# Two-layer MLP behind a short convolution: half-size first weight pieces, a partial band read first, clipping on GpSimd, chunk groups across batches, warming on 64 rows

## The chip, the core and the metric

The program runs on one core of one Trainium2 chip. The metric is the device time of one execution in microseconds (us). Five engines work beside each other and wait for each other through semaphores: TensorE (PE; PEld is its weight load), VectorE (DVE), ScalarE (ACT), GpSimd (POOL) and SyncE (SP), which here only issues DMAs.

## The reference

```python
# x (2, 4096, 192), weight (8, 7): causal convolution of 7 taps, one set of taps per head of 24 columns
w = softmax(weight)
out[b, s, head] = sum_k w[head, k] * x_pad[b, s + k, head]
x = out.reshape(8192, 192)
# layer 1: w_in (192, 2048), w_out (2048, 192)
h = x @ w_in;  x = np.maximum(0.01 * h, h) @ w_out
# layer 2, weights of its own and scalars a[0..3], b[0..1]
h = x @ w_in;  h2 = h * h;  h3 = h2 * h
P = a[0] + a[1] * h + a[2] * h2 + a[3] * h3
Q = 1.0 + np.abs(b[0]) * np.abs(h) + np.abs(b[1]) * h2
result = (P / (Q + 1e-6)) @ w_out
```

The four weight matrices arrive as 64-bit floats and are turned into 32-bit ones on the chip.

## The kernel before

**Tiling.** The 8192 tokens are 16 blocks of 512. The 2048 hidden columns are 16 slices of 128, so each layer has 16 x 16 jobs (block i, slice j). Every product is made exact enough by splitting both factors in a high and a low part: a job has 5 matmuls of 512 columns into one PSUM bank in `gemm1` (main high x main weights high and low, main low x high, and two against `wiR`, which packs the 64 remaining input columns, high on partitions 0 to 63 and low on 64 to 127), then an activation, then 5 matmuls in `gemm2_hi` (3) and `gemm2_lo` (2) into accumulators `acc`. That is 2 x 256 x 10 = 5120 big matmuls. Layer 1's activation is `l1_s`, `l1_hi`, `l1_lo`; layer 2's rational function takes about a dozen steps (`l2_...`) on ACT, DVE and POOL.

**Start.** The softmax of the taps is made on ACT and DVE and written to DRAM with zeros beside it (`s_put`, L343); `s_get` (L348) reads it back skewed as `band`, one 128x128 band matrix for each head, in two reads of four heads. `conv` multiplies the bands with the tokens (`xt`), `conv_evac` and `conv_wrap` copy to `xc`, `trans` (L547) transposes it on PE, and `x_hi`, `x_lo` split it. So blocks 0 and 1 are prepared. For all later blocks `group(g)` convolves chunks of 122 tokens, up to five in a group (`conv_g`, two halves of four heads), stores them to `y_dram` (`put_g`), and `fetch` reads them back turned. There are 6 groups in batch 0 and 7 in batch 1. While the first loads run, `s_warm` (L350) keeps PE busy with 8 matmuls of 256 columns and 19 of 192 to 512 columns on all 128 rows.

**Weights.** They come in 28 pieces: `m` (512 columns of the main 128 rows of w_in, 512 KB), `r` (the remaining 64 rows, 512 KB), `o` (256 rows of w_out, 384 KB). `convert` turns a piece into 32-bit floats: `cv_abs` and `cv_low` on ACT, `cv_clip` (two tensor_scalar instructions, L396 and L397) and `cv_bits` (two) on DVE, then `w_hi` on ACT and `w_lo` on DVE or POOL. An `r` piece goes through a copy by DMA in between (`r_dup`, L431). Layer 1's first pieces are r0, m0 and o0.

**What sets the order.** Every step is entered with a rank: a due time built from constants (`LEAD`, `GAP`, `PREP`, `STEP`, `AHEAD`) plus an offset of its name in the table `OFF`. `Planner.run` then lets engines take steps one by one, by its own costs and the ranks (`PULL`, `WINDOW`, `LOOK`), picks the engine where a step may run on two, and hands out buffers of the pools `bank` (4 PSUM banks), `work`, `pair` and `raw`. The result is one fixed row of instructions for each engine; an engine never passes an instruction that waits. The last block's layer 2 (16 jobs) can only start when its layer 1 and `middle` are done, since each block's layer 2 needs all of layer 1's sum.

In the profile `act`, `stt`, `tt` and `mm` are helpers of one line each, so most steps show as L244 (ACT), L250 and L247 (DVE, POOL) and L253 (PE).

## Time and profile before

| | us |
|---|---|
| median of 3 runs (lowest, highest) | 1245.04 (1243.78, 1246.08) |
| the profiled execution | 1244.22 |
| its span, first to last instruction | 1242.4 |
| PE busy | 1217.3 (98%) |
| ACT, DVE, POOL busy | 1138.5, 1112.0, 1059.2 |
| first big matmul starts | 17.83 |
| last block's layer 2 starts on PE | 1175.03 |

The span is what the profiler saw; 1.8 us of the execution's own time lie around it. A matmul's record is longer than its share of the engine, since matmuls overlap: the distance from one start to the next is what counts. A time in brackets behind a timeline row is how long the engine had been idle before it, and what ended that.

### The profile page before, as it was taken

To read this page: it belongs to the slowest core of one execution; us is meant where nothing else is said; L and a number is where in the kernel's file an instruction comes from. 1 tells how busy PE (TensorE), PEld (TensorE's weight loads), DVE (VectorE), ACT (ScalarE), POOL (GpSimd) and SP (SyncE) were. 2 spreads that over 40 slices of the span, in tenths; PEclk is the share of its full clock that TensorE was granted. 3 is DMA by queue.
4 is the path that set the end of the run, shared out by engine and by line. 5 is a ranking of instruction groups with operands and counts; after the bars stand their busy time and mean duration, and the time that the engine had idled before them with its cause. 6 is when DMAs were issued, how large, how long until landed. Compare 5 with 4: busy or idle time off the path is not lost.

```text
span 1242.4 us, 17891 instructions
## 1 busy us (share of the span) xinstructions
PE 1217.3 (98%) x5437; PEld 997.6 (80%) x5437; DVE 1112.0 (90%) x1671; ACT 1138.5 (92%) x1996; POOL 1059.2 (85%) x1000
## 2 busy tenths in 40 slices
PE   8999999999999999999999999999999999999976
PEld 7787788888888888888888888888888888888744
DVE  7999989898998989898988999898998989889898
ACT  6889999899999999999999999999999999999996
POOL 2787988989889898898888989899898888988886
PEclk9999999999999999999999999999999999999998
DMA  7752002020110201111010111010210002000000
GB/s 210 200 164 71 1 3 52 2 42 1 38 18 1 56 1 44 18 30 33 7 45 12 29 33 29 20 23 5 50 26 1 13 1 41 1 1 14 1 13 13
DMA packets 137414, 42.34 MB, mean 34 GB/s; under 512 B 113571, under 2 KB 134758, under 8 KB 137318
## 3 DMA queue, kind: packets, MB, share of 16 engines
q1 hardware_dynamic: 135702, 41.00, 14.3%
q8 instruction: 42, 0.69, 0.2%
q14 instruction: 54, 0.44, 0.1%
q10 hardware_dynamic: 1616, 0.21, 0.1%
HBM read 27.28 MB, written 11.80 MB: 31 GB/s over the span
## 4 chain that ended last, share of the span: by engine, by line
PE 81%; ACT 7%; DVE 7%; issue 2%; DMA 1%; POOL 1%; SPq 0%; POOLq 0%; DVEq 0%; ACTq 0%
PE bank L253 41%; PE acc L253 39%; ACT work L244 4%; DVE work L250 2%; ACT raw L244 1%; DMA raw<-in_moe_w_in_dram 1%; DVE bank L250 1%; DVE pair L247 1%; ACT bank L244 1%; DVE bank L396 1%; DVE bank L397 1%; DVE pair L250 1%; DVE work L247 0%; DVE raw L250 0%; POOL pair L247 0%
## 5 line engine op out<-in xcount | busy, mean ns | idle before, releaser
L253 PE MATMUL acc<-pair,wo 128*128 128x512 f32 x2560 | 657.4, 391 | 6.2 <-POOL pair L247 2.7
L253 PEld LDWEIGHTS acc<-pair,wo 128*128 128x128 f32 x2560 | 478.5, 188 | 110.6 <-POOL pair L247 6.9
L244 ACT ACTIVATE work<-work 128x512 f32<-128x512 f32 x532 | 331.4, 630 | 17.6 <-DVE work L250 11.0
L247 POOL TENSOR_TENSOR work<-work,pair 128x512 f32<-128x512 f32 x184 | 239.5, 1302 | 43.6 <-DVE pair L250 34.6
L253 PE MATMUL bank<-xh,wiH 128*128 128x512 f32 x512 | 203.5, 397 | 9.2 <-DVE raw L250 4.2
L253 PE MATMUL bank<-xh,wiL 128*128 128x512 f32 x512 | 200.2, 391 | 0.0
L253 PE MATMUL bank<-xl,wiH 128*128 128x512 f32 x512 | 200.0, 391 | 0.0
L253 PE MATMUL bank<-xl,wiR 128*128 128x512 f32 x512 | 200.0, 391 | 0.0
L253 PE MATMUL bank<-xh,wiR 128*128 128x512 f32 x512 | 199.9, 390 | 0.0
L250 DVE SCALAR_TENSOR_TENSOR work<-work,b_sb,bank 128x512 f32<-128x512 f32 x182 | 135.1, 742 | 46.5 <-ACT work L244 45.3
L247 POOL TENSOR_TENSOR pair<-work,work 128x512 fp32r<-128x512 f32 x122 | 158.0, 1297 | 20.4 <-DVE work L250 14.8
L250 DVE SCALAR_TENSOR_TENSOR work<-bank,a_sb,work 128x512 f32<-128x512 f32 x184 | 136.9, 744 | 9.6 <-POOL work L247 7.6
L244 ACT ACTIVATE work<-bank,a_sb 128x512 f32<-128x512 f32 x176 | 135.3, 769 | 6.1 <-PE bank L253 6.0
L250 DVE SCALAR_TENSOR_TENSOR pair<-bank,a_sb,work 128x512 fp32r<-128x512 f32 x168 | 125.2, 745 | 13.1 <-ACT work L244 7.8
L250 DVE SCALAR_TENSOR_TENSOR bank<-work,a_sb,bank 128x512 f32<-128x512 f32 x176 | 132.1, 752 | 4.1
L244 ACT ACTIVATE raw<-raw 128x512 f32<-128x512 f32 x202 | 126.8, 630 | 6.2 <-DVE raw L250 3.6
L253 PEld LDWEIGHTS bank<-xh,wiH 128*128 128x128 f32 x512 | 96.4, 188 | 38.1 <-DVE raw L250 6.6
L247 POOL TENSOR_TENSOR pair<-work,pair 128x512 fp32r<-128x512 f32 x92 | 120.3, 1308 | 7.0 <-PE acc L253 1.8
L244 ACT ACTIVATE work<-bank,b_sb 128x512 f32<-128x512 f32 x182 | 124.0, 681 | 0.0
L247 DVE TENSOR_TENSOR work<-work,bank 128x512 f32<-128x512 f32 x176 | 119.3, 678 | 1.3 <-ACT raw L244 1.3
L253 PEld LDWEIGHTS bank<-xl,wiH 128*128 128x128 f32 x512 | 96.5, 189 | 20.7 <-DVE xl L247 0.3
L253 PEld LDWEIGHTS bank<-xl,wiR 128*128 128x128 f32 x512 | 96.4, 188 | 20.6 <-DVE xl L247 0.3
(104 smaller groups left out, 1954.5 us busy)
## 6 DMA issues: line engine op xcount, KB each, us to landing
work<-y_dram SPq DMA_DIRECT2D x108, 64.0 KB
raw<-in_moe_w_out_dram SPq DMA_DIRECT2D x16, 384.0 KB
...
```

The source lines that it names most:

```text
L244: nc.scalar.activation(out=out_, in_=in_, func=func, **k)
L247: (eng or nc.vector).tensor_tensor(out=out_, in0=in0, in1=in1, op=op)
L250: nc.vector.scalar_tensor_tensor(out=out_, in0=in0, scalar=s, in1=in1, op0=op0, op1=op1)
L253: nc.tensor.matmul(out=out_, lhsT=w, rhs=r, start=start, stop=stop)
L396: nc.vector.tensor_scalar(out=a, in0=a, scalar1=F64_TINY, scalar2=F64_HUGE, op0=ALU.max, op1=ALU.min)
L397: nc.vector.tensor_scalar(out=ai, in0=ai, scalar1=3, scalar2=0x3FFFFFF8, op0=ALU.logical_shift_left, op1=ALU.bitwise_and)
```

## The change

What it does:
- **First pieces in halves.** Layer 1's r0 and m0 are replaced by `h0`, `h1` (256 columns of the main rows each, 256 KB) and `d0`, `d1`, `d4`, `d5` (256 columns of the remaining rows, read twice by DMA onto both halves of the partitions, so that no copy between is needed). They are loaded into `work` buffers. `gemm1` of the first two jobs is cut in `gemm1_main` (3 matmuls) and `gemm1_rest` (2), which are ranked apart.
- **Band.** Only the 112 x 103 part of each band that blocks 0 and 1 need is read first, one half issued by SP and one by ACT; the full bands are read again later (two reads of 256 KB). All weight pieces from the fifth on, block 1's tokens and the scalars are held until the taps are in DRAM (`gate`).
- **Conversion.** The first instruction of `cv_clip` may run on POOL or DVE; the shift is a step of its own (`cv_shift`). The PSUM bank is taken from the shift on, before it was taken from `cv_abs` on.
- **First convolution.** The copy of the second half goes to DVE, the wrap to POOL, and the first transpose no longer waits for the wrap.
- **Groups.** Chunks are grouped in fives across the batch border: 12 groups of 5, where there were 13 of 4 or 5.
- **Warming.** 6 matmuls of 256 columns and 16 of 512; 11 of the 16 use 64 rows (8 on either half in turn, 3 on the lower).
- **Ranks.** All constants and the table `OFF` have other numbers. Two rows of it: `'gemm2_lo': -4.32` becomes `-10.85`, `'l2_r': 2.84` becomes `-69.14`. They re-deal the order of the whole program.

```diff
@@ constants
-LEAD = 66.057
-GAP = 6.373
-PREP = 56.276
+LEAD = 56.215
+GAP = -6.556
+PREP = 24.574
-WARM = 8
-SHAPES = ((192, 6, 1), (384, 3, 1), (512, 3, 1), (256, 3, 1), (192, 4, 0))
+WARM = 6
+SHAPES = (("full", 3), ("both", 8), ("low", 3), ("full", 2))
-STEP = 4.016
-PULL = 0.005
-WINDOW = 193.974
-LOOK = 58
+STEP = 3.163
+PULL = 0.002
+WINDOW = 201.705
+LOOK = 127
...
+START = (-83.5, -81.0, -70.0, -69.0, -68.0)
+COORD = (-215.4, -14.15, -250.79, 88.2, 44.65)
@@ chunks and groups
-    groups = []
+    chunks = []
     for bi in range(B):
-        t0 = max(blocks[DIRECT][3] - bi * S, 0) if bi == 0 else 0
-        count = -(-(S - t0) // CG)
...
+        t0 = blocks[DIRECT][3] if bi == 0 else 0
+        while t0 < S:
+            s0 = min(t0, S - CG)
+            chunks.append((bi, s0, t0 - s0))
+            t0 = s0 + CG
+    groups = [chunks[c:c + NTC] for c in range(0, len(chunks), NTC)]
@@ band, warming, loads
-    def s_get(eng, m):
+    def s_get(eng, m, rows, cols):
...
+        (nc.scalar if eng == "ACT" else nc.sync).dma_start(out=band[0:rows, m * HB:(m + 1) * HB, P - cols:P], in_=src)
-        for cols, count, step in SHAPES:
+        for part, count in SHAPES:
             for n in range(count):
-                k = n * step % 4
-                mm(acc[0][1][:, 0:cols], t[:, k * P:(k + 1) * P], t[:, 0:cols], True, True)
+                k = n % 4
+                half = n % 2 if part == "both" else 0
+                a, z = (0, P) if part == "full" else (half * R, (half + 1) * R)
+                mm(acc[0][half], t[a:z, k * P:(k + 1) * P], t[a:z], True, True)
+        elif kind == "h":
+            nc.sync.dma_start(out=t.bitcast(I32)[:, 0:FB], in_=w_ins[l][0:P, q * FB:(q + 1) * FB])
+        elif kind == "d":
+            for half in range(2):
+                nc.sync.dma_start(out=t.bitcast(I32)[half * R:(half + 1) * R, 0:FB], in_=w_ins[l][P:D, q * FB:(q + 1) * FB])
@@ conversion
-        ai = a.bitcast(I32)
-        nc.vector.tensor_scalar(out=a, in0=a, scalar1=F64_TINY, scalar2=F64_HUGE, op0=ALU.max, op1=ALU.min)
-        nc.vector.tensor_scalar(out=ai, in0=ai, scalar1=3, scalar2=0x3FFFFFF8,
+        (nc.gpsimd if eng == "POOL" else nc.vector).tensor_scalar(out=a, in0=a, scalar1=F64_TINY, scalar2=F64_HUGE,
+                                                                  op0=ALU.max, op1=ALU.min)
+
+    def cv_shift(eng, l, kind, q, n):
+        nc.vector.tensor_scalar(out=buf[("cb", l, kind, q)].bitcast(I32)[:, 0:n],
+                                in0=buf[("cq", l, kind, q)].bitcast(I32)[:, 0:n], scalar1=3, scalar2=0x3FFFFFF8,
                                 op0=ALU.logical_shift_left, op1=ALU.bitwise_and)
@@ convolution of the first block
     def conv_wrap(eng, i):
-        pv = conv_view(buf[("cps", i, 1)], blocks[i][2])
-        nc.vector.tensor_copy(out=xc[0:CT, 0:pv.shape[1], D:D + R], in_=pv[:, :, HC - R:HC])
+        nc.gpsimd.tensor_scalar(out=xc[0:CT, :, D:D + R], in0=xc[0:CT, :, D - R:D], scalar1=1.0, scalar2=0.0,
+                                op0=ALU.mult, op1=ALU.add)
@@ order of the pieces, ranks
+    seq0 = [("h", 0), ("d", 0), ("h", 1), ("d", 1), ("o", 0), ("o", 1), ("r", 1), ("m", 1), ("o", 2), ("o", 3), ("d", 4),
+            ("m", 2), ("d", 5), ("o", 4), ("o", 5), ("m", 3), ("o", 6), ("o", 7)]
-    pieces = [(0,) + p for p in seq] + [(1,) + p for p in seq]
+    pieces = [(0,) + p for p in seq0] + [(1,) + p for p in seq]
...
+           load_w, l, kind, q, r=["gate"] if n >= 4 else [], w=[key], take=("work" if small else "raw", key), extra=FIRST if n < 2 else DMA_LAND + 1.2 * (n < 6),
...
-    on(ACT(0.4), -82, 0, s_put, r=["taps"], w=["tdram"], extra=2.4)
+    on(ACT(0.4), -100, 0, s_put, r=["taps"], w=["tdram"], extra=2.4)
+    on(SP(0, 0.1), -99.5, 0, lambda eng: None, r=["tdram"], w=["gate"])
     for m in range(2):
-        on(SP(0, 1), -82, 0.1, s_get, m, r=["tdram"], w=[("band", m)], extra=3.3)
+        on(ACT(0.5) if m else SP(0, 1), -100, 0.1 * m, s_get, m, -(-CR // 16) * 16, CT, r=["tdram"],
+           w=[("band", h) for h in range(m * HB, (m + 1) * HB)], extra=2.9)
...
-        on(DVE(2 * t_dve(w, 1)), c, 0.2, cv_clip, *a, w, r=[cq], w=[cq])
+        on(POOL(t_pool1(w)) + DVE(t_dve(w)), c, 0.2, cv_clip, *a, w, r=[cq], w=[cq])
+        on(DVE(t_dve(w)), c, 0.25, cv_shift, *a, w, r=[cq], w=[cb], take=("bank", cb))
...
-            on(PE(t_pe(n, 5)), s, 0.00, gemm1, *k, r=x_keys(0, i) + w1_keys(0, j), w=[h], take=("bank", h))
+            if i == 0 and j < 2:
+                xk, wk = x_keys(0, i), w1_keys(0, j)
+                on(PE(t_pe(n, 3)), s, 0.00, gemm1_main, *k, r=xk[0::2] + wk[:2], w=[h], take=("bank", h))
+                on(PE(t_pe(n, 2)), s, 0.00, gemm1_rest, *k, r=xk[1::2] + wk[2:], w=[h])
+            else:
+                on(PE(t_pe(n, 5)), s, 0.00, gemm1, *k, r=x_keys(0, i) + w1_keys(0, j), w=[h], take=("bank", h))
...
     for i in range(2):
         layer1(i)
         middle(i)
+        if i == 1:
+            for m in range(2):
+                on(SP(P * HB * P * 4, 1), 30, 0.1 * m, s_get, m, P, P, r=["tdram", ("gH", 0, 1, 1)],
+                   w=[("band", h) for h in range(m * HB, (m + 1) * HB)], extra=3.3)
         prep(i + 1)
```

Three places in the instruction rows. The names: `bank`, `acc` are PSUM; `xh`, `xl` are the high and low part of a block's input (79, 81: block 0); `wiH`, `wiL`, `wiR` and `wo` the weights (68 to 74 layer 1, 69 to 75 odd numbers layer 2); `raw`, `work` and `pair` are SBUF buffers; DMAHW0 to 7 are the eight semaphores that DMAs signal in turn, so that a DMA also waits for the one that had its semaphore before.

ACT at the start, before: the write of the taps waits for DVE alone; a conversion begins behind it.

```order
3 L244 ACTIVATE wsm<-wsm 8x7 [waits DVE_49]
4 L343 DMA taps_dram<-work_103 8x256 [waits DVE_49]
5 L244 ACTIVATE bank_99<-raw_126 128x512 [waits DMAHW2_49,DMAHW1_49]
6 L244 ACTIVATE work_104<-raw_126 128x512
7 L244 ACTIVATE bank_100<-raw_127 128x512 [waits DMAHW1_49]
8 L244 ACTIVATE work_106<-raw_127 128x512
9 L244 ACTIVATE b_sb<-b_sb 128x2 [waits DMAHW0_49]
10 L244 ACTIVATE xc<-bank_101 103x5x96 [waits PE_49]
11 L244 ACTIVATE xc<-bank_102 103x5x96 [waits PE_49]
```

ACT at the start, now (work_104 holds h0, 106 h1, 105 d0):

```order
3 L247 ACTIVATE wsm<-wsm 8x7 [waits DVE_49]
4 L344 DMA taps_dram<-work_103 8x256 [waits DMAHW1_49,DVE_49]
5 L247 ACTIVATE work_108<-work_104 128x256
6 L247 ACTIVATE work_109<-work_104 128x256
7 L349 DMA band<-taps_dram 112x4x103 [waits DMAHW5_49,DMAHW1_49]
8 L247 ACTIVATE wiH_68<-work_109 128x256 [waits DVE_49]
9 L247 ACTIVATE work_110<-work_106 128x256 [waits DMAHW2_49]
10 L247 ACTIVATE work_111<-work_106 128x256
11 L247 ACTIVATE wiH_68<-work_111 128x256 [waits DVE_49]
12 L247 ACTIVATE work_112<-work_105 128x256 [waits DMAHW7_49,DMAHW0_49]
13 L247 ACTIVATE work_113<-work_105 128x256
14 L247 ACTIVATE xc<-bank_101 103x5x96 [waits PE_49]
```

The write of the taps now waits for the load of h0 too (its semaphore, DMAHW1: row 5 reads h0 and needs no wait of its own any more), and a DMA that waits for that write's landing stands ahead of all but one of the conversions.

PE at the first big matmuls, before: ten in a row, jobs 0 and 1 whole.

```order
17 L253 MATMUL acc_96<-qc,ident 128x256
18 L253 MATMUL bank_101<-xh_79,wiH_68 128x512
19 L253 MATMUL bank_101<-xh_79,wiL_70 128x512
20 L253 MATMUL bank_101<-xl_87,wiH_68 128x512
21 L253 MATMUL bank_101<-xh_81,wiR_72 128x512
22 L253 MATMUL bank_101<-xl_89,wiR_72 128x512
23 L253 MATMUL bank_100<-xh_79,wiH_68 128x512
24 L253 MATMUL bank_100<-xh_79,wiL_70 128x512
```

PE at the first big matmuls, now:

```order
19 L256 MATMUL bank_99<-xt_77,band 103x5x24 x4
20 L256 MATMUL bank_100<-xh_79,wiH_68 128x512
21 L256 MATMUL bank_100<-xh_79,wiL_70 128x512
22 L256 MATMUL bank_100<-xl_87,wiH_68 128x512
23 L256 MATMUL bank_101<-xh_79,wiH_68 128x512
24 L256 MATMUL bank_101<-xh_79,wiL_70 128x512
25 L256 MATMUL bank_101<-xl_87,wiH_68 128x512
26 L256 MATMUL bank_99<-xt_77,band 103x5x24 x4
27 L256 MATMUL acc_96<-qc,ident 128x256 x2
28 L256 MATMUL bank_100<-xh_81,wiR_72 128x512
29 L256 MATMUL bank_100<-xl_89,wiR_72 128x512
30 L567 MATMUL bank_99<-ident,xc 128x103 x4
```

The main parts of both jobs stand ahead of block 1's second convolution, and the products with `wiR` behind it.

PE where the last block's layer 1 ends, before (row 4496 is its last matmul; pair with wo_75 is layer 2 of the block before, xh_84 the last block's layer 2):

```order
4496 L253 MATMUL acc_95<-pair_124,wo_74 128x512
4497 L253 MATMUL acc_97<-pair_121,wo_75 128x512 x2
4498 L253 MATMUL acc_98<-pair_121,wo_75 128x512
4499 L253 MATMUL acc_98<-pair_119,wo_75 128x512
4500 L253 MATMUL acc_97<-pair_119,wo_75 128x512
4501 L253 MATMUL acc_97<-pair_118,wo_75 128x512 x2
4502 L253 MATMUL acc_98<-pair_118,wo_75 128x512
4503 L253 MATMUL acc_98<-pair_120,wo_75 128x512
4504 L253 MATMUL acc_97<-pair_120,wo_75 128x512
4505 L253 MATMUL acc_97<-pair_116,wo_75 128x512 x2
4506 L253 MATMUL acc_98<-pair_116,wo_75 128x512
4507 L253 MATMUL bank_102<-xh_84,wiH_69 128x512
```

The same place now (the last block's layer 1 ends with row 4494, four rows above the first that is shown; the rows between are five matmuls of the same kind):

```order
4498 L256 MATMUL acc_97<-pair_120,wo_75 128x512
4499 L256 MATMUL acc_97<-pair_117,wo_75 128x512 x2
4500 L256 MATMUL acc_98<-pair_117,wo_75 128x512
4501 L256 MATMUL acc_98<-pair_118,wo_75 128x512
4502 L256 MATMUL acc_97<-pair_118,wo_75 128x512
4503 L256 MATMUL acc_97<-pair_125,wo_75 128x512 x2
4504 L256 MATMUL acc_98<-pair_125,wo_75 128x512
4505 L256 MATMUL acc_98<-pair_122,wo_75 128x512
4506 L256 MATMUL acc_97<-pair_122,wo_75 128x512
4507 L256 MATMUL acc_97<-pair_119,wo_75 128x512 x2
4508 L256 MATMUL acc_98<-pair_119,wo_75 128x512
4509 L256 MATMUL bank_101<-xh_84,wiH_69 128x512
```

Between the last block's layer 1 and its layer 2 PE has 18 matmuls of the block before where it had 13. Behind the last block's `middle` DVE has 88 instructions in both rows.

## Rows read from the trace of the kernel before

**Rows 1.** The page: span, busy time of PE, chain by engine.

```profile
span 1242.4 us, 17891 instructions
...
PE 1217.3 (98%) x5437; PEld 997.6 (80%) x5437; DVE 1112.0 (90%) x1671; ACT 1138.5 (92%) x1996; POOL 1059.2 (85%) x1000
...
PE 81%; ACT 7%; DVE 7%; issue 2%; DMA 1%; POOL 1%; SPq 0%; POOLq 0%; DVEq 0%; ACTq 0%
```

**Rows 2.** Stretches: length, busy PE, PEld, DVE, ACT, POOL, clock, DMA share, GB/s.

```profile
2.10:9.50 7.40, 7.00 (x27) 5.98 (x28) 3.91 (x11) 1.94 (x4) 0.34 (x1) 1.00 0.87 244
...
60.00:1170.00 1110.00, 1108.22 (x4970) 915.44 (x4969) 999.26 (x1489) 1034.53 (x1810) 975.90 (x916) 1.00 0.12 26
1170.00:1242.40 72.40, 54.14 (x198) 37.00 (x197) 63.55 (x96) 60.42 (x102) 55.84 (x49) 0.93 0.07 11
```

**Rows 3.** Chain of waits, one dense piece: start, us, what.

```profile
236.77 2.27 PE bank L253 x10
```

**Rows 4.** Timeline of PE around one group: start, us, instruction, count.

```profile
488.59 1.04 PE L253 MATMUL bank<-xt,band 128*122 128x120 f32 x8
489.39 1.41 PE L253 MATMUL acc<-pair,wo 128*128 128x512 f32 x5
490.63 1.01 PE L253 MATMUL bank<-xt,band 128*122 128x120 f32 x8
491.41 0.47 PE L253 MATMUL bank<-xh,wiH 128*128 128x512 f32 x1
```

**Rows 5.** Timeline of the start, all engines.

```profile
2.50 5.70 PE L253 MATMUL acc<-qc,ident 128*128 128x256 f32 x16 [2.50 <-POOL ident masks.py:199]
...
3.67 0.28 ACTq L343 DMA_DIRECT2D taps_dram<-work  x1
...
5.64 0.63 ACT L244 ACTIVATE bank<-raw 128x512 f32<-128x512 f32 x1 [2.79 <-DMA raw<-in_moe_w_in_dram]
...
7.05 0.94 SPq L348 DMA_DIRECT2D band<-taps_dram  x2
...
12.22 2.09 PE L253 MATMUL bank<-xt,band 109*103 109x120 f32 x16 [1.36 <-DMA b_sb<-in_moe_b_dram]
...
13.24 0.87 PEld L253 LDWEIGHTS bank<-xt,band 109*103 109x103 f32 x8 [0.18 <-DMA band<-taps_dram]
...
16.05 1.08 ACT L244 ACTIVATE xh<-bank 128x512 fp32r<-128x512 f32 x2
...
17.83 0.58 PE L253 MATMUL bank<-xh,wiH 128*128 128x512 f32 x1
...
21.81 1.91 PE L253 MATMUL acc<-qc,ident 128*128 128x256 f32 x8
```

**Rows 6.** Timeline of PE, a later stretch.

```profile
34.67 0.39 PE L253 MATMUL bank<-xh,wiH 128*128 128x512 f32 x1
```

**Rows 7.** The page: the DMA queue that SP feeds; packets, MB, share of 16 engines.

```profile
q1 hardware_dynamic: 135702, 41.00, 14.3%
```

**Rows 8.** Timeline of the end, PE and DVE.

```profile
1169.81 5.38 PE L253 MATMUL acc<-pair,wo 128*128 128x512 f32 x23
1175.03 0.39 PE L253 MATMUL bank<-xh,wiH 128*128 128x512 f32 x1
...
1191.91 0.63 PE L253 MATMUL bank<-xh,wiL 128*128 128x512 f32 x1
1192.34 0.63 PE L253 MATMUL bank<-xl,wiH 128*128 128x512 f32 x1
...
1175.43 0.68 DVE L247 TENSOR_TENSOR xl<-work,xh 128x512 fp32r<-128x512 f32 x1
...
1178.21 0.74 DVE L250 SCALAR_TENSOR_TENSOR work<-work,b_sb,bank 128x512 f32<-128x512 f32 x1
1179.76 0.75 DVE L250 SCALAR_TENSOR_TENSOR work<-bank,a_sb,work 128x512 f32<-128x512 f32 x1 [0.81 <-POOL work L247]
...
1236.92 0.72 DVE L699 STREAM_TRANSPOSE work<-acc 128x512 f32<-128x512 f32 x1 [0.83 <-PE acc L253]
```

More of the change, by code (lines that the diff above doesn't have):

```diff
@@ L411, in w_hi @@
         a = buf[("cv", l, kind, q)]
-        if kind == "m":
+        if kind in "hd":
+            act((wiH if kind == "h" else wiR)[l][:, q * HFB:(q + 1) * HFB], a[:, 0:HFB])
+        elif kind == "m":
             act(wiH[l][:, q * FB:(q + 1) * FB], a)
@@ L463, in load_x @@
         load_rows(t, 0, ntc - 1, x[b, r0:r0 + CR, :], CR)
[L465 to L466 removed]
     def load_g(eng, g):
[L469 removed]
         t = xt[g % 2]
[L471 removed]
+        for c, (bi, s0, _) in enumerate(groups[g]):
             if s0 == 0:
@@ L492, in put_g @@
     def put_g(eng, g):
-        bi, starts, t0 = groups[g]
-        for c, s0 in enumerate(starts):
-            rows = s0 + CG - (t0 + c * CG)
+        for c, (bi, s0, done) in enumerate(groups[g]):
+            rows = CG - done
             r0 = B * S - bi * S - s0 - CG
@@ L532, in conv_evac @@
         ntc = -(-n // CT)
-        act(xc[0:CT, 0:ntc, m * HC:(m + 1) * HC], pv, ACTF.Copy)
+        to = xc[0:CT, 0:ntc, m * HC:(m + 1) * HC]
+        if eng == "DVE":
+            nc.vector.tensor_copy(out=to, in_=pv)
+        else:
+            act(to, pv, ACTF.Copy)
         if m == 1 and i:
@@ L754, in load_piece @@
         key = ("raw", l, kind, q)
-        on(SP(P * FB * 8, 2 if kind == "r" else 1), -80 + 3.0 * n if n < 3 else coord[n] - 8.0, 0, load_w, l, kind, q,
-           r=[("cv", 0, "r", 0)] if n == 2 else (), w=[key], take=("raw", key),
-           extra=FIRST if n < 3 else DMA_LAND, retire=(key, "work", halves) if n >= len(pieces) - 3 else None)
+        small = kind in "hd"
+        on(SP(P * FB * (4 if small else 8), 2 if kind in "rd" else 1), START[n] if n < len(START) else coord[n] - 8.0, 0,
+           load_w, l, kind, q, r=["gate"] if n >= 4 else [], w=[key], take=("work" if small else "raw", key), extra=FIRST if n < 2 else DMA_LAND + 1.2 * (n < 6),
+           retire=(key, "work", halves) if n >= len(pieces) - 3 else None)
     def halves(t):
@@ L764, in conv_leaky_rational_kernel @@
         coord[n] = due(l, kind, q) - (CV1 if l == 0 else 0.0)
-    coord[0], coord[1], coord[2] = -76.0, -75.0, -62.0
+    for n, v in enumerate(COORD):
+        coord[n] = v
     c = CV2
-    for n in range(14, 28):
+    for n in range(N0, len(pieces)):
         coord[n] = min(coord[n] - 12.0, c)
@@ L812, in w1_keys @@
     def w1_keys(l, j):
-        return [("wH", l, "m", j // 4), ("wL", l, "m", j // 4), ("wr", l, (j % 8) // 4, j // 8)]
+        main = ("h", j // 2) if l == 0 and j < 4 else ("m", j // 4)
+        rest = [("wL", l, "d", j // 2)] if l == 0 and j % 8 < 4 else [("wr", l, (j % 8) // 4, j // 8)]
+        return [("wH", l) + main, ("wL", l) + main] + rest
     def x_keys(l, i):
@@ L836, in fetch @@
         base = t1[i * NJ] - AHEAD
-        yk = [("y", g) for g, (bi, starts, t0) in enumerate(groups)
-              if bi * S + t0 < tok0 + n and bi * S + starts[-1] + CG > tok0]
+        yk = [("y", g) for g, (a, z) in enumerate(spans) if a < tok0 + n and z > tok0]
         for m in range(2):
@@ L851, in prep @@
         if i >= DIRECT:
-            while made[0] < len(groups) and groups[made[0]][0] * S + groups[made[0]][2] < blocks[i][3] + blocks[i][2]:
+            while made[0] < len(groups) and spans[made[0]][0] < blocks[i][3] + blocks[i][2]:
                 group(made[0])
@@ L860, in prep @@
         base = t1[i * NJ]
-        c = [base - PREP + STEP * k for k in range(4)] if i else [-83.0] * 4
-        if i >= 2 and blocks[i][1] == 0:
-            on(DVE(0.25), base - 66, 2.0, zero_x, i, w=[("xt", p)])
-        on(SP(P * ntc * D * 4, 3), max(base - 66, 4) if i else -81, 2.0, load_x, i, w=[("xt", p)],
+        c = [base - PREP + STEP * k for k in range(4)] if i else [-100.0] * 4
+        on(SP(P * ntc * D * 4, 3), 4 if i else -83.4, 0.0, load_x, i, r=["gate"] if i else [], w=[("xt", p)],
            extra=DMA_LAND if i else 3.3)
@@ L971, in conv_leaky_rational_kernel @@
     on(POOL(0.01), -84, 0, lambda eng: None, w=["spare"])
-    for n in (0, 1):
-        convert(n)
     prep(0)
-    for n in range(2, len(pieces)):
+    convert(0)
+    for n in range(1, len(pieces)):
         load_piece(n)
```

109 lines of the change are left out of this document (57 added, 52 removed).

## Prediction

> **What bounds the kernel now.** I read the page first: PE is busy for 1217.3 of 1242.4 us and has 81% of the chain that ended last [rows 1]. Then the stretches. From 60 to 1170 us PE is busy for 1108.2 of 1110 us at the full clock, and every other engine has 75 us and more to spare [rows 2]. Ten big matmuls there take 2.27 us, start to start, so one costs 0.227 us [rows 3], and the 5120 of them 1162 us. So 80 us of the span are not big matmuls, and only these can be saved. They lie in three places. The start: the first big matmul begins at 17.83 us [rows 5]. The middle: the 4970 records of 60 to 1170 us [rows 2] are 192 of convolution groups (12 groups of 16) and 4778 big ones. These are worth 4778 x 0.227 = 1084.6 us; a group costs 0.80 us for each half (488.59 to 489.39, and 490.63 to 491.41 [rows 4]), 1.58 us in all, 12 of them 19.0 us; the rest, 1110 - 1084.6 - 19.0 = 6.4 us, is stalls. The end: in the last 72.4 us PE is busy for 54.1 only and DVE for 63.6 [rows 2]; the last block's rational function on DVE sets the pace there.
>
> **The change part by part.**
>
> *Groups.* 13 become 12, and a group's price is 1.58 us on PE, which nothing else hides in the dense middle [rows 4]: **-1.6 us**. Bounds: PE waits for nobody there, so the whole 1.6, or nothing if the freed time turns into a stall.
>
> *The start.* The first convolution waits for the bands: they were issued at 7.05 us, the first four heads' matmuls began at 12.22, and the next four's weights at 13.24, on the landing of the second read [rows 5]. Now for what changes this. (a) The write of the taps went out at 3.67 us; now it also waits for h0. The first piece of 512 KB had landed at 5.64 [rows 5]; at 244 GB/s [rows 2] its second half is 1.05 us of that, so h0, half as large, lands at about 4.6. The write landed by 7.05 at the latest, 3.4 us after its issue, since the read behind it did not wait; so the taps are in DRAM at 4.6 + 3.4 = 8.0 at the latest, and I take 7.5. (b) Ahead of the band then lie 1470 KB (h0, h1, d0, d1 and block 0's tokens), where it was 1940 KB, and the band itself is 2 x 184 KB where it was 512. From 2.1 us on at 244 GB/s 1837 KB are through at 9.6, against 2.1 + 10.0 = 12.1 for 2450 KB before. Before, the second half's matmuls began 1.1 us behind that sum, so now 9.6 + 1.1 = 10.7, and from the other side 7.5 + 3.4 = 10.9. I take 11.0 for both halves. The eight heads' products run one behind the other (16 records in 2.09 us): from 11.0 to 13.0, where they ended at 13.24 + 0.9 = 14.1. Gain there 1.1 us. (c) ACT is the next thing late: it issues its half of the band at 7.5 and is then behind with eight ACTIVATEs of 256 columns, two of 384, a copy and a small one, two of them waiting for DVE's bits and the copy for the convolution. A dense ACTIVATE of 512 columns goes 0.54 us apart (1.08 for two [rows 5]); the short ones I take at 0.3 to 0.45, so it reaches `xh` at about 14.6 to 15.0 instead of 16.05, and the first big matmul comes at about 16.1 instead of 17.83. (d) Behind it the products with wiR wait for d0's conversion, the first second halves (`gemm2_hi`) for o0, block 1's transposes for ACT's copies. By the new PE row, jobs 0 and 1 are through at 24.8 us, then six first halves and their second halves follow with no other work between, and the 51st big matmul comes at about 31.6. Before it came at 34.67 [rows 6], with a convolution group (1.6) ahead that now comes later: 33.1. So the start is worth **-1.5 us**. Bounds: 0, if the band or ACT is no earlier than before; -3, if the waits at jobs 0 and 1, about 3.9 us before (33.1 - 17.83 - 50 x 0.227), shrink by half as well.
>
> *The full bands* are read again, 512 KB at 244 GB/s = 2.1 us of queue time. The order has them ahead of the first group's matmuls by some 7 us of PE work, which hides it; without that cover it would cost up to 2.1 us.
>
> *Clipping.* An instruction of about 0.6 us moves from DVE to POOL for 18 of the 32 pieces. They lie early in the dense part, beside PE's work: counted at nothing, hidden by DVE's spare time, and worth at most a share of the 6.4 us of stalls.
>
> *The end.* Behind the last block's `middle` DVE has the same 88 instructions as before, so the end lasts as long as they do, from the first one that needs the last block's job 0. Before, layer 1 ended 13 matmuls ahead of 1175.03 (23 records from 1169.81, ten of them ahead: 1172.1), the last low part was made at 1175.43, and DVE began job 0 at 1178.21 [rows 8]. Now 18 matmuls stand between instead of 13. Layer 1 ends 5 x 0.227 = 1.1 us sooner, but job 0 waits for 18 x 0.227 = 4.1 us of PE work, where it started 2.9 us behind: 1.1 - 0.9 leaves **-0.2 us**. Bounds: DVE idles 8.9 us in this stretch [rows 2], a part of it 0.81 us behind POOL [rows 8]; the new order may take 2 us of that or add 2.
>
> *Other ranks.* All of the middle is dealt anew. Its stalls are 6.4 us; I take them as unchanged, with -3 and +3 as the ends that one order of this kind can differ from another.
>
> Sum: -1.6 - 1.5 - 0.2 = **-3.3 us**. On the profiled execution (1244.22, of which the span is 1242.4 and 1.8 lie around it) that gives 1240.9; the median of the runs stands 0.8 higher, so 1241.7 on that. I forecast **1241.3 us**.
>
> **A rule against it.** The whole queue's 135702 packets, 302 bytes on average, take 14.3% of 16 engines' span, 21 ns for each [rows 7]; so packets smaller than a band row are cheap here. The Trainium skill (DMA: Bandwidth & Descriptors, Specifications) says that a transfer wants 512 bytes to run at line rate, and that below it the engine reads, modifies and writes; a band row is now 412 bytes where it was 512. By that rule the smaller read would be no quicker than the old one, and the sum -1.8 instead of -3.3. The row speaks against it.
>
> **The rivals.**
> 1. *The new order does more.* Half of the stalls of the middle (3.2 us of 6.4) and 1 us of DVE's idle time at the end go as well: 1241.3 - 4.2 = 1237.1. For it: every engine but PE has slack in the middle, so a better order can exist, and DVE loses work to POOL. Against: 6.4 us in 1110 are few already.
> 2. *The start gives nothing.* The band comes no earlier than before: the write waits for h0, the packets are small, and ACT, which issues half of the band, holds all its conversions but two behind that wait. If the taps land at 9.3 us instead of 7.5, the first big matmul is back at 17.83. Then only the group and the end are left, -1.8: 1242.8. If the freed time of the group is lost too, 1244.6. This is also the case in which the change does not do what it says.
> 3. *Slower: the end grows.* In the last block DVE, ACT and POOL are all nearly full (63.6, 60.4 and 55.8 of 72.4 us [rows 2]), and a wait of DVE there is paid in full. The order of all steps there is new; if DVE waits for POOL or ACT 0.5 us more in each of 16 jobs, that is +8 us: 1249.3. From 3.3 us on it eats the gain, from 5.8 on the kernel is measurably slower. For it: waits of up to 0.81 us stand there already, twice the clock fell in that stretch (matmuls 0.43 us apart, 1.2 GHz, at 1192 [rows 8]) after PE had waited. Against: the loads of the engines are the same, and PE has slack there.
> 4. *Slower: the warming on 64 rows does not hold the clock.* Fills went 5.70 / 16 = 0.36 us apart at the start and 1.91 / 8 = 0.24 later [rows 5], so the clock rose while PE warmed. If half rows don't keep it up, big matmuls cost 0.43 instead of 0.227 [rows 8] until it rises: 8 us at the low level are 8 x (1 - 0.227/0.43) = 3.8 us lost. 1245.
>
> **How the numbers follow.** A measurement of this kernel can tell about 0.2%, 2.5 us, from no change: faster is below 1242.55, slower above 1247.5. The forecast (1239.5 to 1243) 0.44, of which 0.06 lie above 1242.55; rival 1 0.22; rival 2 (1242.6 to 1247) 0.21; rival 3 0.09, of which 0.07 is slower; rival 4 0.04, of which 0.01 is slower. Faster 0.38 + 0.22 = 0.60; slower 0.08; within 0.06 + 0.21 + 0.02 + 0.03 = 0.32. The range from 1237.0 to 1246.0 holds the forecast, half of rival 1, nearly all of rival 2 and part of 3 and 4: 0.44 + 0.11 + 0.20 + 0.05 = 0.80.
>
> **What would show it.** Groups: 192 convolution records of groups plus 32 of blocks 0 and 1, 224 instead of 240. The start: the first band matmul near 11.0 us, both halves with no wait between; `xh` near 15; the first big matmul near 16.1, the 51st near 31.6. If the write of the taps starts at its old 3.67, step (a) is wrong. The clock: fills and big matmuls 0.24 and 0.23 us apart behind 11 us. The end: DVE's first instruction of the last block's job 0 58.7 us ahead of its transpose of the last block's sum, as before (1178.21 to 1236.92 [rows 8]). What would make the prediction wrong is a difference between 32 and 1170 us above 3 us other than the group, or an end that differs by more than 2 us.

## The result

The kernel after takes 1255.57 us (median, 1254.87 to 1257.1), the kernel before 1244.84 in the same comparison: a ratio of 1.0088, 95% interval 1.0070 to 1.0105. It is 11 us slower, where 3.3 us faster was forecast.

The page of the kernel after, the lines that answer to [rows 1]: PE has as much to do as before, in a longer span; less of the chain lies on DVE and some more on POOL.

```profile
span 1253.8 us, 17893 instructions
...
PE 1219.7 (97%) x5412; PEld 994.6 (79%) x5412; DVE 1116.8 (89%) x1694; ACT 1133.4 (90%) x2002; POOL 1072.9 (86%) x999
...
PE 81%; ACT 6%; DVE 4%; POOL 2%; issue 1%; DMA 1%; POOLq 0%; DVEq 0%; SPq 0%; ACTq 0%
```

The stretches of the kernel after (length, busy time of PE, PEld, DVE, ACT, POOL with counts, granted clock, DMA share, GB/s), as in [rows 2], with one more from 30 to 140 us:

```profile
30.00:140.00 110.00, 100.18 (x438) 78.21 (x437) 93.48 (x150) 89.33 (x172) 94.43 (x88) 1.00 0.49 131
60.00:1170.00 1110.00, 1102.70 (x4922) 906.33 (x4921) 999.58 (x1504) 1024.06 (x1801) 965.18 (x893) 1.00 0.12 27
1170.00:1253.80 83.80, 65.52 (x251) 48.17 (x249) 73.53 (x111) 68.13 (x117) 67.31 (x60) 0.92 0.06 10
```

The same stretch of the kernel before:

```profile
30.00:140.00 110.00, 107.93 (x475) 86.49 (x474) 102.26 (x167) 99.94 (x188) 88.06 (x95) 1.00 0.45 125
```

From 30 to 140 us PE issues 37 matmuls fewer than before. DVE and ACT are less busy too; POOL alone does more, 94.4 us instead of 88.1. So DVE and ACT, which feed PE, wait for something, and POOL is the one engine that has more to do. The waits of the kernel after in this stretch say for what (engine, line, releaser: us in all, times, longest):

```profile
DVE bank L407 <- POOL work L403: 9.8, 11, 1.9
ACT wiH L247 <- DVE work L253: 7.8, 5, 2.7
ACT wo L247 <- DVE work L253: 7.8, 8, 1.5
PEld bank L256 <- DVE work L253: 7.2, 9, 1.4
PEld bank L256 <- DVE pair L250: 6.2, 4, 2.3
```

L403 is the clip, L407 the shift behind it. DVE works its queue in order: while the shift waits for GpSimd's clip, everything behind it waits too, ACT's high parts of the weights and PE's operands among it. The groups of the same stretch on POOL show why (columns, form, count; busy, mean ns):

```profile
L403 POOL TENSOR_SCALAR work<-work 128x512 f32<-128x512 f32 x6 | 12.0, 1993 | 1.1 <-ACT work L247 0.8
L403 POOL TENSOR_SCALAR work<-work 128x384 f32<-128x384 f32 x8 | 11.9, 1488 | 0.4
L641 POOL TENSOR_SCALAR pair<-work 128x512 fp32r<-128x512 f32 x18 | 11.4, 634 | 5.5 <-ACT work L247 3.1 <-PE bank L256 1.1 <-issue 0.5
```

A clip of 512 columns takes 1.99 us on GpSimd in the mean, not 0.6. L641 is a multiply-add with one input of the same size: 0.63. The planner prices both alike (`t_pool1`: 0.161 + n/1200, 0.588 for 512), so all 18 clips were dealt as if they were done after a third of their time. Above the planner's price lie 7 x 1.4 + 9 x 1.0 + 2 x 0.7 = 20 us of POOL that the order does not know of.

A small table of what the traces give, for the kernels spoken of below. All columns but the last are of the profiled execution, which can stand some us off the median (clip_light's took 1246.9 us, clip_psum's 1246.7). "Stall" is what two big matmuls stand apart beyond 0.227 us with no convolution between them, "conv" the same with one between; "tail" runs from the 4801st big matmul to the span's end; all in us. From 30 to 140 us the kernels in the order of the change have two groups where the others have one, 1.6 us of "conv".

| kernel | first / 51st big matmul | 30-140 stall, conv | 140-1170 stall, conv | tail | median |
|---|---|---|---|---|---|
| before | 17.83 / 34.67 | 4.5, 1.8 | 3.4, 17.6 | 102.1 | 1244.1 to 1244.8 |
| after | 18.05 / 34.34 | 12.1, 6.2 | 6.4, 15.9 | 101.7 | 1255.6 |
| clip_light | 18.18 / 33.52 | 4.7, 4.3 | 6.5, 15.9 | 101.9 | 1244.4 |
| clip_psum | 17.27 / 33.02 | 7.5, 5.9 | 5.2, 15.9 | 99.0 | 1248.4 |
| warm_rows | 16.96 / 32.23 | 5.9, 4.4 | 6.4, 15.9 | 99.4 | 1244.3 |
| groups_alone | 17.98 / 35.01 | 4.1, 1.9 | 5.7, 16.2 | 102.1 | 1245.5 |
| ranks | 17.64 / 33.72 | 5.5, 1.5 | 4.3, 16.5 | 100.0 | 1242.3 |

### The profile page after: what moved, and what is told of

The parts are those of the page before. It is cut to its first block, busy times and chain, and to the rows that moved or that the text cites. A ratio compares the mean times of both kernels' runs of the same rounds, so it can differ in the third digit from the quotient of the medians.

```text
span 1253.8 us, 17893 instructions
## 1 busy us (share of the span) xinstructions
PE 1219.7 (97%) x5412; PEld 994.6 (79%) x5412; DVE 1116.8 (89%) x1694; ACT 1133.4 (90%) x2002; POOL 1072.9 (86%) x999
## 4 chain that ended last, share of the span: by engine, by line
PE 81%; ACT 6%; DVE 4%; POOL 2%; issue 1%; DMA 1%; POOLq 0%; DVEq 0%; SPq 0%; ACTq 0%
PE bank L256 42%; PE acc L256 40%; ACT work L247 3%; ACT raw L247 2%; DVE work L253 1%; DVE bank L253 0%; POOL work L403 0%; DVE pair L253 0%; POOL pair L250 0%; DMA work<-work 0%; ACT pair L247 0%; DVE work L250 0%; ACT bank L247 0%; DVE raw L253 0%; DMA raw<-in_moe_w_out_dram 0%
## 5 line engine op out<-in xcount | busy, mean ns | idle before, releaser
L256 PE MATMUL acc<-pair,wo 128*128 128x512 f32 x2560 | 646.2, 391 | 6.3 <-POOL pair L250 3.2
L247 ACT ACTIVATE work<-work 128x512 f32<-128x512 f32 (+2 forms) x531 | 322.6, 625 | 18.8 <-DVE work L253 11.6
L250 POOL TENSOR_TENSOR work<-work,pair 128x512 f32<-128x512 f32 x177 | 234.3, 1325 | 44.3 <-DVE pair L253 38.1
L253 DVE SCALAR_TENSOR_TENSOR work<-bank,a_sb,work 128x512 f32<-128x512 f32 x177 | 132.0, 746 | 26.0 <-POOL work L250 24.5
L253 DVE SCALAR_TENSOR_TENSOR work<-work,b_sb,bank 128x512 f32<-128x512 f32 x175 | 129.7, 741 | 24.8 <-ACT work L247 24.5
L253 DVE SCALAR_TENSOR_TENSOR pair<-bank,a_sb,work 128x512 fp32r<-128x512 f32 x173 | 128.6, 746 | 11.6 <-PE acc L256 5.7
L250 POOL TENSOR_TENSOR pair<-work,pair 128x512 fp32r<-128x512 f32 x88 | 116.8, 1327 | 11.5 <-PE acc L256 6.6
L247 ACT ACTIVATE work<-bank,b_sb 128x512 f32<-128x512 f32 x175 | 119.4, 683 | 0.0
L250 POOL TENSOR_TENSOR raw<-raw,pair 128x512 f32<-128x512 f32 x78 | 101.2, 1297 | 18.0 <-DVE pair L253 15.0
L256 PEld LDWEIGHTS bank<-xh,wiR 128*128 128x128 f32 x512 | 96.4, 188 | 21.6 <-POOL wiR L250 1.1
```

Source lines behind the costliest of these rows:

```text
L247: nc.scalar.activation(out=out_, in_=in_, func=func, **k)
L250: (eng or nc.vector).tensor_tensor(out=out_, in0=in0, in1=in1, op=op)
L253: nc.vector.scalar_tensor_tensor(out=out_, in0=in0, scalar=s, in1=in1, op0=op0, op1=op1)
L256: nc.tensor.matmul(out=out_, lhsT=w, rhs=r, start=start, stop=stop)
```

## The experiments

**1. The clip's length, order kept (clip_light).** Theory "price": the clip's length on GpSimd is the loss. Rivals: the hand-over to a third engine, or the new order.

```diff
-tensor_scalar(out=a, in0=a, scalar1=F64_TINY, scalar2=F64_HUGE, op0=ALU.max, op1=ALU.min)
+tensor_scalar(out=a, in0=a, scalar1=1.0, scalar2=0.0, op0=ALU.mult, op1=ALU.add)   # GpSimd's 18
```

> The kernel after, with the 18 clips that GpSimd was dealt written as a multiply by 1.0 and an add of 0.0 in place of the max and min (so those pieces are not clipped); every instruction keeps its place on its engine. In the trace of the kernel after, the max and min on GpSimd takes 1.99 us for 512 columns and 1.49 for 384, its multiply-add 0.63 for 512 (L641), and DVE stood 11.1 us, 12 times, waiting for a clip. Theory 'price' (the clip's length on GpSimd is what makes the kernel slower): clips of about 0.5 to 0.65 us, DVE's waits for them below 3 us in all, time 1244 to 1247, where the kernel after takes 1255.6. Rival 'hand-over' (a third engine in each conversion's chain costs by itself, however short its instruction): 1252 to 1256. Rival 'order' (the ranks dealt anew are the loss): 1253 to 1256.

Measured: 1244.41 us, ratio to before 1.0001 (0.9987 to 1.0014). Its trace, the clip's line (min/median/max ns, forms; who waited for it: us, times):

```profile
L404 POOL TENSOR_SCALAR work<-work x18: 407/521/798, 15.8 to 117.3; 128x384 f32<-128x384 f32 x9, 128x512 f32<-128x512 f32 x7, 128x256 f32<-128x256 f32 x2
...
  DVE bank L407: 1.1, 3
```

Same order, same hand-over, a third of the length: the 11 us are gone, and DVE's waits for the clip with them (1.1 us, 3 times; 11.1, 12 times in the kernel after, over the whole span). "Price" holds; "hand-over" and "order" fall as causes of the loss. But the 3.3 us of the forecast are not there either.

**2. What of the clip is long (clip_forms, one run).** Diff: GpSimd's 18 clips alternately as max+min, max+add 0, multiply by 1+min, max+multiply by 1.

> One look at what makes the clip long on GpSimd: the kernel after, dealt as it was, with GpSimd's 18 clips in four forms by piece: max and min; max and add of 0; multiply by 1 and min; max and multiply by 1 (the last three clip on one side only). If the two-sided compare is the cost, the one-sided forms take 0.5 to 0.65 us for 512 columns like a multiply-add; if any compare is, they all take 1.9 to 2.0; if each compare adds its share, 1.2 to 1.3.

Measured: 1255.87 us, and no form is shorter than another:

```profile
L407 POOL TENSOR_SCALAR work<-work x18: 1069/1504/2183, 18.0 to 128.8; 128x384 f32<-128x384 f32 x9, 128x512 f32<-128x512 f32 x7, 128x256 f32<-128x256 f32 x2
```

The seven of 512 columns took 1.91 to 2.18 us, the nine of 384 columns 1.49 to 1.51. One compare is as long as two: with a max or a min in it the instruction takes about 3.9 ns for each column (3.7 to 4.3 here).

**3. The clip on DVE, dealt again (clip_dve); GpSimd's clip at its true price, dealt again (clip_priced).**

```diff
-on(POOL(t_pool1(w)) + DVE(t_dve(w)), c, 0.2, cv_clip, ...
+on(DVE(t_dve(w)), c, 0.2, cv_clip, ...                        # clip_dve
+on(POOL(0.0039 * w) + DVE(t_dve(w)), c, 0.2, cv_clip, ...     # clip_priced
```

> The kernel after, with the planner allowed only DVE for the clip; the order is dealt again under the same ranks. Theory 'price': no waits of DVE for GpSimd's clips, 1244 to 1247; DVE gets 18 instructions of 0.56 to 0.95 us back (10 to 14 us), which its spare time in the dense part must hold. Rival 'hand-over': the same 1244 to 1247. Rival 'order': 1253 to 1256. If DVE's own time binds between 30 and 140 us, 1249 to 1252.

> The kernel after, with the planner told what a clip on GpSimd takes (0.0039 us per column, 2.0 us for 512, where it counted 0.59); it now deals 10 of the 32 clips to GpSimd in place of 18. Theory 'price': the planner keeps the long clips off the chains that are late, 1244 to 1248. Rival 'hand-over': 10 of 18 waits are left, 1249 to 1252. Rival 'order': 1253 to 1256.

Measured: 1254.16 (1.0080, 1.0065 to 1.0094) and 1291.17 (1.0382, 1.0361 to 1.0402). Theory "price" missed both times: clip_dve's time is the one that rival "order" gave, clip_priced's lies outside every range. In clip_dve no clip is on GpSimd, and 30 to 140 us are as good as in clip_light (stall 3.9, conv 4.4); the loss is elsewhere, 13.6 us of stalls behind 140 us. 5.7 of them lie around 495 us: 3.5 where PE waits twice for DVE's rational function, the rest where the granted clock then reads 0.50 and big matmuls stand 0.43 us apart (waits of 480 to 500 us):

```profile
PEld bank L256 <- DVE raw L253: 2.0, 1, 2.0
PEld acc L256 <- DVE pair L253: 2.0, 1, 2.0
```

In clip_priced 37.8 us of stalls lie between 140 and 400 us. A changed price deals every step behind it anew, and a deal under ranks that were chosen for other prices cost 10 and 47 us here. So a run with a new deal does not tell what a part is worth; from here on the order is kept wherever it can be.

**4. The clip on DVE, order kept (clip_moved), and into PSUM (clip_psum).**

```diff
-(nc.gpsimd if eng == "POOL" else nc.vector).tensor_scalar(out=a, in0=a, ...clip...)
+nc.vector.tensor_scalar(out=a, in0=a, ...clip...)                  # clip_moved
+nc.vector.tensor_scalar(out=cb, in0=a, ...clip...)  # clip_psum: in cv_shift, ahead of the shift; cb is its PSUM bank
```

> The kernel after, dealt as it was, but each of the 18 clips that GpSimd was dealt is issued on DVE at the same place of the order (all else stays). It parts two readings of the planner's-choice run (1254.2 with the clip on DVE and the order dealt again): theory 'price' says that there the new deal lost the time (one stretch at 490 us stood 5.7 us still), so here, without a new deal, 1244 to 1248; DVE gets 18 instructions of about 0.6 us, 10 us, in a stretch where it was 12% idle. Rival 'DVE is full' (the clip was put on GpSimd because DVE has no room for it): 1251 to 1255 again.

> The kernel after, dealt as it was, with every clip made by DVE just ahead of its shift, from the SBUF tile into the PSUM bank that the shift takes anyway (GpSimd makes none). In the run with the clip moved to DVE as it stood (SBUF to SBUF) the 32 clips took 17.1 us: 0.29, 0.35 and 0.42 us for 256, 384 and 512 columns where GpSimd was idle, up to 1.45 where it was at work. Theory 'DVE's SBUF clip waits for GpSimd': written to PSUM they take 0.43, 0.56 and 0.70 each, none above 0.75, the sum 18 us, and with no wait in DVE's queue the stalls of 30 to 60 us fall from 4.8 to 1 to 3; time 1245 to 1248. Rival 'DVE is full there': the sum of the clips is no shorter, so 1248 to 1251 as with the clip moved. Both are far below the 1255.6 of the kernel after.

Measured: 1250.05 (1.0038, 1.0023 to 1.0052) and 1248.43 (1.0037, 1.0023 to 1.0051). The clip's line in clip_moved, then in clip_psum (min/median/max ns):

```profile
L403 DVE TENSOR_SCALAR work<-work x32: 281/417/1445, 4.7 to 157.7; 128x384 f32<-128x384 f32 x16, 128x512 f32<-128x512 f32 x10, 128x256 f32<-128x256 f32 x6
```

```profile
L406 DVE TENSOR_SCALAR bank<-work x32: 417/552/695, 4.6 to 158.6; 128x384 f32<-128x384 f32 x16, 128x512 f32<-128x512 f32 x10, 128x256 f32<-128x256 f32 x6
```

From SBUF to SBUF a clip of 384 columns takes 0.35 us on DVE while GpSimd is idle, and up to 1.45 while GpSimd is at work; into PSUM it takes 0.55 to 0.56 always. The Trainium skill (SBUF — State Buffer, Who interferes with whom) says that DVE and GpSimd share a pair of SBUF ports, that a `tensor_scalar` in DVE's two-port mode takes the pair for its whole length, and that the later of the two waits. These rows agree: the SBUF clips of 384 columns that took longer than 0.36 all ran beside GpSimd's work, and those into PSUM were never longer.

So the change had moved the clip's tile from PSUM, where it took 0.55 to 0.56 us whatever GpSimd did, to SBUF, where some of the 14 clips that were left to DVE wait for GpSimd. That is not the bulk of the loss: clip_light has it too. And without it clip_psum still stands 4 us above clip_light, within the range that "DVE is full" gave. Its stalls of 30 to 60 us fell as the other theory said (2.2 us, 4.8 in clip_moved), but 1.5 of the 4.8 come from the clock, which read 0.50 in clip_moved from 57 to 60 us, behind 2.2 us in which PE waited; and over 30 to 140 us the two kernels lose the same (7.5 and 5.9 in clip_psum, 7.8 and 5.6 in clip_moved). So no gain of the write to PSUM shows, and in this order 18 more clips on DVE are not free. Either way the clip costs: 11 us on GpSimd, 4 to 6 us back on DVE.

**5. Merged groups alone (groups_alone).** The diff is the change's lines on `chunks`, `groups` and `spans`, put into the kernel before.

> The kernel before with one part of the change alone: chunk groups across the batches, 12 instead of 13, everything else as before. By the forecast's step, minus 1.6 us (16 convolution matmuls at full clock): 1243.2. If the freed time turns into a stall: 1244.8. Under the theory 'order', that any new deal of the planner may move the stalls: 1242 to 1248.

Measured: 1245.49, 1.0010 (1.0001 to 1.0018), so 1.2 us slower. 16 convolution matmuls fewer, and conv of 140 to 1170 us falls from 17.6 to 16.2; stall rises from 3.4 to 5.7. Where a group had stood from 565.23 us on (see [rows 4] for one like it), PE now waits for what the next first half needs:

```profile
565.68 0.19 PEld L253 LDWEIGHTS bank<-xh,wiH 128*128 128x128 f32 x1 [1.54 <-DVE work L250]
565.68 0.50 PE L253 MATMUL bank<-xh,wiH 128*128 128x512 f32 x1 [1.12 <-DVE work L250]
```

**6. The start: longer warming (warm_long), whole rows (warm_rows), the band's halves exchanged (band_swap).** All three on clip_light, order kept.

```diff
-SHAPES = (("full", 3), ("both", 8), ("low", 3), ("full", 2))
+SHAPES = (("full", 3), ("both", 8), ("low", 3), ("full", 8))   # warm_long
+SHAPES = (("full", 16),)                                       # warm_rows
-(nc.scalar if eng == "ACT" else nc.sync).dma_start(out=band[...
+(nc.scalar if (eng == "ACT") == (cols == P) else nc.sync).dma_start(out=band[...   # band_swap
```

> The run with the light clip, dealt as it was, with 22 warming matmuls in place of 16 behind the first six (the six more on 128 rows, 0.23 us each). In that run the warming ended at 10.48 us, PE then idled 1.70 us until the bands came, and the granted clock read 0.50 (the level of 1.2 GHz) from 14 to 16 us: two fills took 1.07 us and ten transposes 1.68, where the kernel after, whose warming ended at 11.34, read 1.00 and took 0.60 and 1.12. Theory 'warming too short': no 0.50 behind 12 us, transposes 1.1 us, first big matmul at 17.3 to 17.5 in place of 18.18, time 0.7 to 1 us below the light clip's 1244.4. Rival 'the first product waits for DVE's low parts anyway': first big matmul at 18.0 to 18.2, same time.

> The run with the light clip, dealt as it was, with all 16 later warming matmuls on 128 rows (it had 11 of them on 64 rows); the same number. Rival 4 of the forecast (half rows don't hold the clock): the granted clock reads 1.00 from 10 to 17 us, first big matmul at 17.3 to 17.6, time 0.5 to 1 us lower than the light clip's 1244.4. Against it, theory 'the idle time ahead of the bands': the clock holds during the warming with 64 rows too (1.00 from 2 to 13 us), and falls behind the 1.7 us in which PE has nothing; then nothing changes here, 1244 to 1245, and the clock falls in this run as well if the bands come late.

> The run with the light clip, dealt as it was, with the two halves of the band's first read exchanged between the queues: ACT's queue now fetches the heads that PE needs first. In the kernel after, ACT's half moved from 7.07 to 9.76 us and SP's from 8.70 to 11.31, and PE began at 12.14, behind SP's half. Theory 'two queues share the engines, and the half that PE needs first was put on the later one': first convolution at 10.6 to 11.2 in place of 12.14, second half at 12.1 without a wait of its own, first big matmul up to 1 us sooner, time 0.5 to 1 us lower. Rival 'the bound is the sum of the bytes': the second half is late instead, the transposes are where they were, same time within 0.3 us.

Measured: 1244.26 (1.0002, 0.9993 to 1.0012), 1244.27 (0.9997, 0.9987 to 1.0007), 1244.66 (1.0007, 0.9998 to 1.0016): none differs from clip_light. Theory "warming too short" got its clock, but not its time, and its first big matmul came later than it said (17.77, since PE waited for the tokens until 12.91). The traces show more than the times. Stretches of clip_light (the granted clock is the third number from the end):

```profile
13.00:14.00 1.00, 1.00 (x9) 1.00 (x8) 0.00 (x0) 0.73 (x2) 0.00 (x0) 0.66 1.02 350
14.00:15.00 1.00, 1.00 (x6) 0.77 (x4) 0.34 (x1) 1.00 (x5) 0.00 (x0) 0.50 1.22 325
15.00:16.00 1.00, 1.00 (x5) 0.57 (x4) 0.90 (x3) 0.44 (x2) 0.59 (x2) 0.50 0.90 174
```

PE had idled for 1.70 us ahead of the bands, and its clock then read 0.50, the level of 1.2 GHz. In warm_rows and warm_long PE idled 0.47 and 1.07 us, the clock read 1.00 throughout, and the first big matmul came at 16.96 and 17.77 instead of 18.18. The rows did not do it: the kernel after and clip_psum warm with the same 64-row matmuls as clip_light, PE idled 0.80 and 0.95 us ahead of the bands, and their clock read 1.00 from 10 to 21 us. Nor do rows or idle time alone tell when it falls: hold_end (below) warms on 128 rows, idled 1.18 us and read 0.50 from 14 to 16 us, where the kernel before idled 1.36 and read 1.00. What does stays open.

A held clock pays little: of warm_rows' 1.2 us at the first big matmul the stalls of 30 to 140 us take 1.2 back (5.9 for 4.7).

In band_swap the exchanged half did not come sooner: ACT's queue moved its last band packet at 11.62 us, SP's at 11.74 (10.53 and 11.39 in clip_light). The time is the one of rival "sum of the bytes"; its transposes were to stay where they were, but came 1.2 us later (16.62), with the clock at 0.50 from 13 to 16 us.

**7. What mends the kernel after (mend).** clip_psum with warm_long's `SHAPES`.

> The kernel after, dealt as it was, with the clip on DVE into PSUM and six more warming matmuls on 128 rows. It keeps all of the change but the clip's engine. If the two mended causes are all, it is 0.5 us below the run with the clip into PSUM alone and near 1245; it beats the kernel before (1244.2) only if the start's gain of 1.5 us that was forecast shows, which no run so far has shown: by that 1243.

Measured: 1247.76 (1.0032, 1.0020 to 1.0044), 0.7 us below clip_psum, where 0.5 was expected, but not near 1245: the two causes are not all, and the two mends don't beat the kernel before.

**8. The clock at the end (hold_end), groups under new ranks (ranks), both (best).** On the kernel before.

```diff
-FEED = (('gH', 13), ('h', 14), ('h', 15), ('gH', 15))
+FEED = tuple((t, j) for j in range(13) for t in ('gH', 'gL')) + (('gH', 13), ...   # hold_end, best
-LEAD = 66.057
+LEAD = 66.18        # ranks, best: groups_alone, with PREP 72.588, LOOK 145, OFF and the rest of the table new too
```

> The kernel before with 26 more filling matmuls (256 columns, 0.24 us each) in the last block, each behind a high or a low part of jobs 0 to 12, so that PE does not idle for 1 to 2.2 us there. In runs of one order the last 320 big matmuls and the rest took 99.1 us where the granted clock stayed at 1.00 and 101.7 to 103.2 where it fell to 0.5 for a few us; before, with falls to 0.66 and 0.71, 102.1. Theory 'the clock of the end is paid': clock 1.00 in nearly all of the last 70 us, 1.5 to 2.5 us less there, median 1242.0 to 1243.0 against 1244.2 to 1244.6 of before, and executions nearer to each other. Rival 'DVE sets the pace there': the clock is held and the time is the same within 0.5 us. Rival 'the fills are in the way': 0.5 to 3 us slower.

> The kernel before with the merged groups alone, as in that run, under other ranks (the table of offsets and the constants dealt anew for this form). Theory 'the wait behind the group belongs to the deal': the dense stretches lose the 2 and the 1 us of stalls that the groups alone had, and the 1.6 us show: 1242.2 to 1243.2. Rival 'merging moves a wait into the open': the stalls are found elsewhere, 1244 to 1246 as with the groups alone (1245.5).

> Both of these: merged groups under the new ranks, and the 26 fills in the last block. If both theories hold, 1240.5 to 1241.5, faster than both kernels; if only the clock's does, 1242 to 1243.5; if neither, 1244 to 1246.

Measured: hold_end 1245.91 (1.0014, 1.0004 to 1.0024); ranks 1242.33 (0.9983, 0.9974 to 0.9992); best 1243.34 (0.9994, 0.9983 to 1.0006). hold_end's theory fell: the clock fell all the same (to 0.66 in 5 us, 40 to 50 us ahead of the last big matmul), and the time is the one of "the fills are in the way"; its tail is 104.1 us, where before has 102.1. So the link between the clock of the end and the tail's 99.0 to 103.2 us (the profiled executions of the nine kernels in the order of the change) stays a coincidence of rows that no run could steer.

best's time lies in the range set for "only the clock's theory holds", which is not what happened: with the fills it stands 1.0 us above ranks.

ranks is 1.9 us faster than before by the medians, where the merged groups were forecast at 1.6, but that is not the groups' gain. The stall of 1.12 us at 565 us is gone, and those behind 140 us are 4.3 instead of 5.7; those of 30 to 140 us are 5.5 instead of 4.1. From 30 to 1170 us stalls and convolutions are 27.8 us in ranks, 27.9 in groups_alone and 27.3 before. What ranks gained lies at the start (the 51st big matmul 0.95 us sooner than before) and in the tail (2.1 us shorter). So the stalls were found elsewhere, as rival "merging moves a wait into the open" said, though its time was wrong. This is the version that beats both kernels; it takes nothing else from the change.

## Why the prediction was wrong

**What bounds the kernel:** right. PE's big matmuls stand 0.227 us apart in every run, and between the first and the last of them every change of time is a stall, a convolution or a stretch at the lower clock.

**Clipping:** here it failed. The forecast counted "an instruction of about 0.6 us" and "nothing, hidden by DVE's spare time". The 0.6 has no row in the prediction and no upper end. It fits a multiply-add on POOL (0.63), an operation that looks alike; the clip measured 1.49 us for 384 columns and 1.99 for 512. At that length DVE's spare time hid nothing: the step that follows the moved one (the shift) stayed on DVE, in order, so each clip had to be ready when its turn came. At the length that was forecast the hiding was right: in clip_light (0.41 to 0.66 us) DVE waited 1.1 us for GpSimd's instruction, and no loss of time shows. So the price is the term that failed, and the two-input row of the same engine (1.3 us for 512 columns) should have stood as its other end. Price of the step: 11.2 us (1255.6 less 1244.4).

**Groups:** count right, 224 records; the price right (0.78 us for each half, 1.63 for a whole group in the kernel after). The bound "nothing if the freed time turns into a stall" is what groups_alone did, and ranks too between 30 and 1170 us.

**The start:** wrong, by its steps. The 51st big matmul came at 34.34, where 31.6 was forecast and before has 33.1 without its group: 1.2 us lost, not 1.5 gained. Its rows, to be held against [rows 5]:

```profile
3.68 0.30 ACTq L344 DMA_DIRECT2D taps_dram<-work  x1
...
5.84 0.34 ACTq L349 DMA_DIRECT2D band<-taps_dram  x1
...
12.14 1.86 PE L256 MATMUL bank<-xt,band 109*103 109x120 f32 x16 [0.80 <-DMA band<-taps_dram]
...
15.51 1.08 ACT L247 ACTIVATE xh<-bank 128x512 fp32r<-128x512 f32 x2
...
16.84 0.56 DVE L407 TENSOR_SCALAR bank<-work 128x384 int32<-128x384 int32 x1 [1.28 <-POOL work L403]
...
17.31 1.28 DVE L250 TENSOR_TENSOR xl<-bank,xh 128x512 fp32r<-128x512 f32 x2
...
18.05 0.50 PE L256 MATMUL bank<-xh,wiH 128*128 128x512 f32 x1 [0.81 <-DVE xl L250]
```

(a) fell: the write of the taps left at 3.68, as before, so h0 had landed by then and not at 4.6. (b) fell: PE could begin with the bands at 12.1, not 11.0. The sum counted 1837 KB in one line; but the later loads shared the engines with the band, and 2.37 MB had gone by at 12 us (209, 241, 255, 193 and 286 GB/s in the five stretches of 2 us from 2 us on). (c) `xh` at 15.5 instead of 14.6 to 15.0; and then the first clip on GpSimd held DVE for 1.28 us ahead of the low parts that the first big matmul needs. With the light clip and the clock held (warm_rows) the 51st comes at 32.2, 0.9 us ahead of the 33.1, in one execution.

**The end:** right. DVE's first instruction of the last block's job 0 stands 58.8 us ahead of its transpose (1189.64 to 1248.48), as forecast (58.7), and the end is as long as before. The term of -0.2 has a slip in its sum: 4.1 us of PE work where it was 2.9 is 1.2 more, not 0.9, so it comes out at 0.

**The rule on small rows:** open. In the trace's packets the 412-byte ones of the band took 24 ns in the median, the 512-byte ones of before 27, so a single small packet was no dearer, as the row said. But their mean was 34 ns against 28, and the 896 of them took 30.7 us of the engines' time where 1024 had taken 29.1: in sum the smaller read was no quicker. That is what the rule gives by which a transfer below 512 bytes loses its rate (the Trainium skill, DMA: Bandwidth & Descriptors, Specifications); the later loads beside the band would give it too, and the median speaks for them. No run parts the two.

**Other ranks, and the rivals:** "-3 and +3" for a new deal was too narrow: deals of nearly the same steps gave -1.9, +1.2, +10 and +47 us, and stalls behind 140 us of 3.4 to 13.6 us in the kernels other than clip_priced. With the clip's length taken out, this is where the gain of the groups went: 6.5 us of stalls behind 140 us in clip_light, 3.4 before. Rival 3 had the right mechanism, DVE waiting for POOL, but at the end, where nothing changed. Rival 4's fall of the clock at the start showed in clip_light, behind idle time, not in the profile of the kernel after with the same half rows, and cost nothing that the medians show.
